# An attention and feed-forward kernel on one Trainium2 core: the second projection of five of six token blocks with w_out as the stationary operand

## The chip, the cores and the metric

The kernel runs on one core of one Trainium2 chip. The metric is the device time of the whole program in microseconds (us); lower is better. TensorE (PE) multiplies matrices: each matmul holds one operand, the stationary one, which a weight load (PEld) brings in, and lets the columns of the other, the moving one, stream past; the sums go to PSUM, which has eight banks of 512 fp32 columns. VectorE (DVE), ScalarE (ACT) and GpSimd (POOL) work on tiles, SyncE (SP) issues most DMA transfers. Each engine runs its own queue in order and waits on semaphores of the others.

## The reference

```python
def _attn_ref(r, k, v, w, u):            # B, H, S, D = 4, 8, 768, 48
    for t in range(S):
        cur = np.einsum('bhd,bhe->bhde', u[None] * kt, vt)
        y[:, :, t] = np.einsum('bhd,bhde->bhe', rt, state + cur)
        state = w[None, :, :, None] * state + np.einsum('bhd,bhe->bhde', kt, vt)

def _moe_ref(x, w_in, w_out):            # x 3072 x 384, w_in 384 x 2048, w_out 2048 x 384
    h = x @ w_in
    g = np.where(h > 0.0, h, np.exp(np.minimum(h, 0.0)) - 1.0)
    return g @ w_out
```

x is y with the heads joined: 3072 tokens (4 sequences of 768) of 384 columns. The output is 3072 x 384, fp32.

## The kernel before

The tokens are cut into six blocks n = 0 to 5 (NCH): 128 tokens of each of the four sequences b, so T = 512 columns a block. The hidden columns are cut into 16 chunks f (NF) of 128. `start` (L303) does the attention of block 0 by an order written out by hand (START, L39); then `run` (L294) makes 96 steps (n, f), each by `step` (L384) in the hand-written order FIRST (block 0, L51) or LATER (the rest, L55). Within an engine the instructions stand in the order in which these lists call them.

A step (n, f) holds:
- `hidden` (L933, "hid"): nine matmuls into one of two PSUM banks `ps_h`: three parts c of the 384 input columns, and for each the products (wh, xh), (wh, xl), (wl, xh), since every fp32 operand is held as two fp32r parts, a rounded one and the rest. The stationary operand is w_in, the moving one has 512 columns.
- `negative` and `elu` (L946, L954; "neg" on ScalarE, "elu" on VectorE), then `split_g` ("gh" on ScalarE, "gl" on VectorE), which give the two parts of g.
- `project` (L967, "proj") of an earlier step: one step back in block 0 and in the first steps of block 1, two later. It makes twelve matmuls, three products for each of the four sequences b: the stationary operand is a 128-token part of g, the moving one has the 384 columns of w_out, and each sequence adds up in a PSUM bank of its own, `acc0` to `acc3`.
- a piece of the attention of block n+1 or n+2: a unit (one sequence of one block) is spread over four steps and more by stages. "A" (`scores`, L686) and "Y" (`outputs`, L792) are its matmuls; "Dp" and "Dq" (`diag_scores`, L702) are products on GpSimd, "pa" and "pb" (`take_scores`, L720) take the scores on VectorE, "dk" and "dr" (L636 to L651) turn PSUM into rk on VectorE, "t" (`turn_blocks`, L581) is a transposition in 32 x 32 blocks on VectorE, "kr" (L668) and "ru" (L653) are products.
- in block 0 also the preparation of weight chunk k = f + 2: "ma" and "mb" (`merge`, `sign`, L535 and L544, VectorE) join the words of two stages into `wide`; "sp" (`split_w`, L555) is one ScalarE copy of 768 columns, w_out (i = 0) and w_in (i = 1) together, into the rounded part `wh`; "r3" (`rest_w`, L559) takes the rest of w_out on GpSimd, "r4d" that of w_in on VectorE. In START, sp:1, rs:0 and rsd:1 are the same operations for chunk 1, chunk 0 and chunk 1's w_out, in that order in the list.

At the end of the step after a block's last projection `store` (L983) empties the four accumulators, two copies on VectorE and two on ScalarE, into `o`, and SyncE issues four transfers of 128 rows of 1,536 bytes each. The last block's four transfers are issued by ScalarE.

PSUM holds `acc0` to `acc3`, two `ps_h` banks and two banks `rw` for the attention (`bank`, L238); in `start` the six banks outside `ps_h` take turns.

## Time and profile before

| | us |
|---|---|
| median of 3 runs (516.57 to 517.32) | 517.2 |
| the profiled execution, device time | 517.24 |
| its span, first to last instruction | 515.4 |

| engine | busy us | share of the span |
|---|---|---|
| PE (matmuls) | 501.9 | 97% |
| DVE | 302.3 | 59% |
| ACT | 257.8 | 50% |
| POOL | 118.8 | 23% |

The granted clock of TensorE was 0.998 of full speed in this execution, so 2.4 GHz nearly throughout. Matmuls overlap, and their ends are modelled; so the time that a matmul takes in a stream is read from the distance of starts in the timeline, not from its listed length. DMA packets filled 45% of the 16 DMA engines' span.

### The profile page before, as it was taken

The page shows a single profiled execution, that of the slowest core. Times are in us where ns is not written, and L with a number is a line of the kernel's source. Part 1 is how long each engine was busy: PE and PEld are TensorE (multiplying, and loading weights), DVE is VectorE, ACT ScalarE, POOL GpSimd, SP SyncE. Part 2 cuts the span into 40 slices and gives each one's busy share as a digit, 9 for nine tenths or more (in the row PEclk, how much of TensorE's full clock was granted, in tenths as well). Part 3 has the DMA queues.
Part 4 walks back from the last instruction along what each step waited for, and adds up shares of the span by engine and source line. Part 5 has one row for each costly group of instructions (what it writes and reads, how often), then busy time and mean ns, then how long its engine had stood idle before and what let it go on. Part 6 is the DMA issues. An engine that isn't in the chain of part 4 may idle for free.

```text
span 515.4 us, 9327 instructions
## 1 busy us (share of the span) xinstructions
PE 501.9 (97%) x3568; PEld 442.1 (86%) x3568; DVE 302.3 (59%) x523; ACT 257.8 (50%) x486; POOL 118.8 (23%) x135
## 2 busy tenths in 40 slices
PE   8989999999999999999999999999999999999995
PEld 6888888978888888888888888888888888999995
DVE  6799999995475465564454654654654542433331
ACT  2279888773553543635535435435445354444442
POOL 7732222243322321303303303122022020000000
PEclk9999999999999999999999999999999999999999
DMA  9996779745643551724614634345266200100001
GB/s 134 209 179 157 168 152 228 152 109 148 123 111 66 96 117 29 185 52 88 135 48 92 132 105 96 80 67 126 51 149 135 62 31 8 50 14 1 0 1 66
DMA packets 105562, 50.92 MB, mean 99 GB/s; under 512 B 80162, under 2 KB 101412, under 8 KB 105508
## 3 DMA queue, kind: packets, MB, share of 16 engines
q1 hardware_dynamic: 104932, 49.44, 44.7%
q10 hardware_dynamic: 576, 0.79, 0.4%
q8 instruction: 30, 0.49, 0.4%
q14 instruction: 24, 0.20, 0.1%
HBM read 35.13 MB, written 13.11 MB: 94 GB/s over the span
## 4 chain that ended last, share of the span: by engine, by line
PE 80%; DVE 6%; DMA 5%; ACT 4%; SPq 3%; issue 1%; POOL 0%; DVEq 0%; ACTq 0%
PE ps_acc L978 35%; PE ps_h L941 33%; PE ps_a L696 4%; PE ps_y L811 4%; DMA stage<-in_moe_w_in_dram 3%; PE ps_y L805 2%; SPq L860 1%; DVE wide L539 1%; DMA raw<-in_k_dram 1%; PE ps_y L825 1%; ACT stage L531 1%; DVE wide L547 1%; PE ps_y L751 1%; DVE ps_h L956 1%; DMA stage<-in_moe_w_out_dram 1%
## 5 line engine op out<-in xcount | busy, mean ns | idle before, releaser
L978 PE MATMUL ps_acc<-wh,g 128*128 128x384 f32 x768 | 215.9, 342 | 0.1
L941 PE MATMUL ps_h<-x,wh 128*128 128x512 f32 (+1 forms) x588 | 180.0, 388 | 0.1
L978 PEld LDWEIGHTS ps_acc<-wh,g 128*128 128x128 f32 x768 | 140.8, 188 | 6.9 <-DVE stage L992 0.8
L978 PE MATMUL ps_acc<-wl,g 128*128 128x384 f32 x384 | 129.8, 338 | 0.0
L956 DVE SCALAR_TENSOR_TENSOR ps_h<-g,ps_h 128x512 f32<-128x512 f32 x96 | 66.7, 695 | 104.9 <-ACT g L951 104.5
L941 PEld LDWEIGHTS ps_h<-x,wh 128*128 128x128 f32 x588 | 107.9, 188 | 16.7 <-DVE ps_h L956 0.4
L941 PE MATMUL ps_h<-x,wl 128*128 128x512 f32 (+1 forms) x294 | 114.2, 389 | 0.0
L950 ACT ACTIVATE g<-ps_h 128x512 f32<-128x512 f32 x96 | 57.6, 600 | 92.4 <-PE ps_h L941 92.4
L964 DVE TENSOR_TENSOR g<-ps_h,g 128x512 fp32r<-128x512 f32 x96 | 66.2, 689 | 39.1 <-ACT g L962 38.5
L962 ACT CAST g<-ps_h 128x512 fp32r<-128x512 f32 x96 | 56.1, 584 | 58.3 <-DVE ps_h L956 58.2
L978 PEld LDWEIGHTS ps_acc<-wl,g 128*128 128x128 f32 x384 | 72.2, 188 | 2.1
L941 PEld LDWEIGHTS ps_h<-x,wl 128*128 128x128 f32 x294 | 55.2, 188 | 11.9
L951 ACT ACTIVATE g<-g 128x512 f32<-128x512 f32 x96 | 60.8, 634 | 3.1
L715 POOL TENSOR_TENSOR a<-ident,diag 128x512 f32<-128x512 f32 x21 | 24.3, 1159 | 125.1 <-DVE diag L666 75.6
L722 DVE COPY_PREDICATED a<-mask,ps_a 128x512 f32<-128x512 int32 x40 | 29.0, 735 | 31.9 <-PE ps_a L696 31.9
L850 ACT CAST x<-ps_y 128x256 fp32r<-128x256 f32 x40 | 13.0, 376 | 66.9 <-PE ps_y L825 51.6
L673 POOL TENSOR_TENSOR k_t<-k_t,rev 128x384 f32<-128x384 f32 x12 | 12.2, 1017 | 109.2 <-PE ps_y L805 80.8
L564 POOL TENSOR_TENSOR wl<-wide,wh 128x384 fp32r<-128x384 f32 x16 | 16.8, 1051 | 46.6 <-ACT wh L557 46.4
L711 ACT ACTIVATE a<-ident,diag 128x128 f32<-128x128 f32 x76 | 24.2, 394 | 0.0
L840 DVE TENSOR_TENSOR state<-sw,ps_y 48x192 f32<-48x192 f32 x32 | 11.2, 351 | 20.1 <-ACT x L850 19.7
L811 PE MATMUL ps_y<-a,v_t 128*64 128x128 f32 x320 | 21.9, 279 | 0.0
L615 POOL TENSOR_TENSOR rk<-rk,pw 128x512 f32<-128x512 f32 x16 | 19.1, 1192 | 8.1 <-DMA rk<-blocks 8.1
(107 smaller groups left out, 420.2 us busy)
## 6 DMA issues: line engine op xcount, KB each, us to landing
blocks<-tb SPq DMA_DIRECT2D x64, 128.0 KB, 2.3
rk<-blocks SPq DMA_DIRECT2D x16, 512.0 KB, 3.5
stage<-in_moe_w_out_dram SPq DMA_DIRECT2D x16, 384.0 KB, 5.0
stage<-in_moe_w_in_dram SPq DMA_DIRECT2D x32, 144.0 KB, 4.5
r_t<-in_r_dram SPq DMA_DIRECT2D x22, 192.0 KB, 4.3
k_t<-in_k_dram SPq DMA_DIRECT2D x22, 192.0 KB, 5.0
v_t<-in_v_dram SPq DMA_DIRECT2D x22, 192.0 KB, 5.3
out_dram<-stage SPq DMA_DIRECT2D x20, 192.0 KB, 2.1
```

The lines of the kernel that those rows point to most:

```text
L696: self.nc.tensor.matmul(pa[i][:, a * P : (a + 1) * P], lhsT=kw[rows, a, :], rhs=rw[rows, a, :], start=True, stop=True,)
L711: self.nc.scalar.activation(un["a"][i][:, a, :], self.ident, AF.Copy, scale=diag[:, a : a + 1])
L715: self.nc.gpsimd.tensor_mul(un["a"][i], self.ident.unsqueeze(1).to_broadcast([P, HP, P]), diag.unsqueeze(2).to_broadcast([P, HP, P]),)
L722: self.nc.vector.copy_predicated(un["a"][i], self.mask.bitcast(I32).unsqueeze(1).to_broadcast([P, HP, P]), un["pa"][i].rearrange("p (a t) ...
L811: nc.tensor.matmul(y, lhsT=v[:, h * D : h * D + DP], rhs=un["a"][h % 2][:, h // 2, :], start=(n == 0 and s == 0), stop=(s == 1), skip_grou ...
L941: self.nc.tensor.matmul(ph[:, part], lhsT=a[:, c * P : (c + 1) * P], rhs=x[:, c, part], start=(c == 0 and i == 0), stop=(c == NC - 1 and i ...
L950: nc.scalar.activation(g, ph, AF.Relu, scale=-1.0)
L951: nc.scalar.activation(g, g, AF.Exp, scale=-1.0)
L956: self.nc.vector.scalar_tensor_tensor(ph, g, -1.0, ph, op0=ALU.add, op1=ALU.max)
L962: nc.scalar.copy(part, g)
L964: nc.vector.tensor_sub(part, g, self.g[n, f][2].bitcast(F32))
L978: self.nc.tensor.matmul(self.acc[n][b][:, 0:DM], lhsT=a[:, at], rhs=w, start=(f == 0 and i == 0), stop=(f == NF - 1 and i == 2),)
```

## The change

The projection of blocks 0 to 4 swaps its operands: a 128-column part of w_out is stationary, g moves with 512 columns. There are three accumulators (one for each 128 output columns) instead of four, nine matmuls a step instead of twelve, and the sums come out with output columns on the partitions. Block 5 (`by_tokens`) keeps the old form, with its fourth accumulator in an `rw` bank. Three `rw` banks take the place of two.

So that a transposition in 32 x 32 blocks on VectorE puts whole runs of 96 output columns together, the columns of w_out are regrouped when it is split: `split_w` becomes a GpSimd copy of w_out (384 columns, runs of 32) and a ScalarE copy of w_in (384 columns). GpSimd's copy stands in its queue where "sp" is called, ahead of Dp, "r3" and, in START, of rs:0. Block 5 reads w_out as the moving operand with the regrouping undone, in runs of 32 columns.

`store` of blocks 0 to 4 is one ScalarE copy of `acc1` (512 columns) to `o_raw`, and three VectorE transpositions of 512 columns: of `acc0`, of `acc2`, and of `o_raw`. The stores go out as sixteen transfers of 48 KB with runs of 384 bytes, four at the end of each of the next four steps (`store_next`).

```diff
     def bank(self, kind):
-        tag, bufs = "rw", 2
+        tag, bufs = "rw", 3
         if self.all_banks:
-            tag = ("rw", "rw", "acc0", "acc1", "acc2", "acc3")[self.bank_n % 6]
-            bufs = 1 if tag.startswith("acc") else 2
+            tag = ("rw", "rw", "rw", "acc0", "acc1", "acc2")[self.bank_n % 6]
+            bufs = 1 if tag.startswith("acc") else 3
...
+        self.store_next()
         if last[1] == NF - 1 and last[0] in self.acc:
             self.store(last[0])
...
     def split_w(self, k):
-        if k <= NF:
-            self.nc.scalar.copy(self.pairs[k][0], self.place(self.wide, k, WIDE).bitcast(F32))
+        if k > NF:
+            return
+        for i, copy in enumerate((self.nc.gpsimd.tensor_copy, self.nc.scalar.copy)):
+            if self.has(k, i):
+                copy(*(self.grouped(t, i) for t in (self.weight(k, i)[0], self.joined(k, i))))
...
+    def grouped(self, t, i):
+
+        if i == 1:
+            return t
+        if t.dtype == F32R:
+            return t.rearrange("p (c i d) -> p c i d", c=NC, i=4)
+        return t.rearrange("p (i c d) -> p c i d", c=NC, i=4)
...
     def project(self, n, f):
...
-        for b in range(B):
-            at = slice(b * P, (b + 1) * P)
+        for j, acc in enumerate(self.acc[n]):
             for i, (a, w) in enumerate(((gh, wh), (gh, wl), (gl, wh))):
+                if by_tokens:
+                    at, lhs = acc[:, 0:DM], a[:, j * P : (j + 1) * P]
+                    rhs = w.rearrange("p (c i d) -> p i c d", c=NC, i=4)
+                else:
+                    at, lhs, rhs = acc, w[:, j * P : (j + 1) * P], a
                 self.nc.tensor.matmul(
-                    self.acc[n][b][:, 0:DM], lhsT=a[:, at], rhs=w,
+                    at, lhsT=lhs, rhs=rhs,
                     start=(f == 0 and i == 0), stop=(f == NF - 1 and i == 2),
                 )
...
+        o = self.o.rearrange("p (j c d) -> p c j d", j=T // 32, c=NC)
+        nc.scalar.copy(self.o_raw, acc[1])
+        for c, src in ((0, acc[0]), (2, acc[2]), (1, self.o_raw)):
+            nc.vector.transpose(o[:, c], src.rearrange("p (j t) -> p j t", t=32))
+        self.to_store = [(n, b) for b in range(B)]
...
+    def store_next(self):
+        if not self.to_store:
+            return
+        n, b = self.to_store.pop(0)
+        o = self.o.rearrange("p (b j d) -> p b j d", b=B, j=4)[:, b]
+        out = self.out.rearrange("(b n j t) (i d) -> n b i t j d", b=B, n=NCH, j=4, i=4)[n, b]
+        for i in range(4):
+            self.nc.sync.dma_start(out[i], o[i * 32 : (i + 1) * 32])
```

## Rows read from the trace of the kernel before

**Rows 1.** The page's first part: busy us, share of the span, instructions of an engine.

```profile
PE 501.9 (97%) x3568; PEld 442.1 (86%) x3568; DVE 302.3 (59%) x523; ACT 257.8 (50%) x486; POOL 118.8 (23%) x135
```

**Rows 2.** Busy time in stretches of 20 us: a stretch of block 0, one of block 2, one of block 5. Columns: length, then busy us (and instructions) of PE, PEld, DVE, ACT, POOL, the granted clock, the DMA share, GB/s.

```profile
80.00:100.00 20.00, 19.62 (x149) 17.11 (x149) 18.83 (x32) 17.77 (x30) 5.62 (x5) 1.00 0.90 180
...
220.00:240.00 20.00, 20.00 (x149) 17.71 (x148) 10.86 (x19) 8.89 (x18) 4.97 (x5) 1.00 0.43 88
...
460.00:480.00 20.00, 20.00 (x103) 18.23 (x102) 6.58 (x10) 8.72 (x15) 0.00 (x0) 1.00 0.00 1
```

**Rows 3.** Timeline of PE in block 5: the first row is the first of a step's twelve projection matmuls, the second the first of the next nine hidden ones, the third the fourth of these, the last the first matmul of the next projection. Columns: start, length, engine, line, operation, count; a row may join several matmuls.

```profile
469.86 0.33 PE L978 MATMUL ps_acc<-wh,g 128*128 128x384 f32 x1
...
471.95 0.62 PE L941 MATMUL ps_h<-x,wh 128*128 128x512 f32 x2
...
472.65 0.62 PE L941 MATMUL ps_h<-x,wh 128*128 128x512 f32 x2
...
474.01 0.33 PE L978 MATMUL ps_acc<-wh,g 128*128 128x384 f32 x1
```

**Rows 4.** Timeline of PE in block 1, a projection that follows attention matmuls (first and second matmul), the hidden matmuls after it, and the next projection.

```profile
128.58 0.44 PE L978 MATMUL ps_acc<-wh,g 128*128 128x384 f32 x1
128.87 0.34 PE L978 MATMUL ps_acc<-wl,g 128*128 128x384 f32 x1
...
130.79 0.63 PE L941 MATMUL ps_h<-x,wh 128*128 128x512 f32 x2
...
132.88 0.33 PE L978 MATMUL ps_acc<-wh,g 128*128 128x384 f32 x1
```

**Rows 5.** Groups of instructions by line and shape, whole span: count, busy us and mean ns of one, idle us of the engine before it and what ended that.

```profile
L564 POOL TENSOR_TENSOR wl<-wide,wh 128x384 fp32r<-128x384 f32 x16 | 16.8, 1051 | 46.6 <-ACT wh L557 46.4
...
L585 DVE STREAM_TRANSPOSE tb<-r_t 128x512 f32<-128x512 f32 x16 | 11.2, 702 | 0.0
...
L134 POOL MEMSET state<- 128x256 f32 x3 | 0.8, 312 | 0.0
...
L504 ACT COPY pwt<-ps_pt 128x512 f32<-128x512 f32 x1 | 0.6, 587 | 0.5 <-PE ps_pt L502 0.5
```

**Rows 6.** Timelines at the ends of blocks 1, 3 and 4: the two VectorE copies of the store, and the PE rows of the first projection of the next block (for block 1's end also the third row, which holds the wait, and the start of what follows).

```profile
211.46 1.01 DVE L992 COPY stage<-ps_acc 128x384 f32<-128x384 f32 x2
...
211.33 0.33 PE L978 MATMUL ps_acc<-wh,g 128*128 128x384 f32 x1
...
211.68 0.83 PE L978 MATMUL ps_acc<-wh,g 128*128 128x384 f32 x2
...
213.75 0.62 PE L941 MATMUL ps_h<-x,wh 128*128 128x512 f32 x2
...
373.01 1.01 DVE L992 COPY stage<-ps_acc 128x384 f32<-128x384 f32 x2
...
373.11 0.33 PE L978 MATMUL ps_acc<-wh,g 128*128 128x384 f32 x1
...
448.39 1.01 DVE L992 COPY stage<-ps_acc 128x384 f32<-128x384 f32 x2
...
449.09 0.33 PE L978 MATMUL ps_acc<-wh,g 128*128 128x384 f32 x1
```

**Rows 7.** Timelines at the end of `start`: "mb" of chunk 1 on VectorE, rs:0 on GpSimd, and the third matmul of the first hidden half on PE, the first one that reads rs:0's result.

```profile
29.74 0.94 DVE L547 SCALAR_TENSOR_TENSOR wide<-stage,wide 128x768 int32<-128x768 int32 x1
...
30.05 1.50 POOL L564 TENSOR_TENSOR wl<-wide,wh 128x384 fp32r<-128x384 f32 x1 [1.51 <-ACT wh L557]
...
32.23 0.29 PE L941 MATMUL ps_h<-x,wl 128*128 128x256 f32 x1
```

**Rows 8.** Timelines of `start` (first three rows: GpSimd, then the same VectorE form twice, first beside that GpSimd product and later without one) and of block 0 around steps (0, 12) and (0, 13): VectorE, GpSimd and PE.

```profile
24.64 1.27 POOL L625 TENSOR_TENSOR a<-a,mask 128x512 f32<-128x512 f32 x1 [1.22 <-ACT a L624]
...
24.71 1.61 DVE L539 SCALAR_TENSOR_TENSOR wide<-stage 128x384 int32<-128x384 int32 x1
...
112.39 0.55 DVE L539 SCALAR_TENSOR_TENSOR wide<-stage 128x384 int32<-128x384 int32 x1
...
101.15 0.94 DVE L547 SCALAR_TENSOR_TENSOR wide<-stage,wide 128x768 int32<-128x768 int32 x1
...
104.41 0.55 DVE L673 TENSOR_TENSOR k_t<-k_t,rev 128x384 f32<-128x384 f32 x1
...
107.44 0.70 DVE L956 SCALAR_TENSOR_TENSOR ps_h<-g,ps_h 128x512 f32<-128x512 f32 x1
...
101.38 1.62 POOL L715 TENSOR_TENSOR a<-ident,diag 128x512 f32<-128x512 f32 x1 [3.11 <-DVE diag L666]
103.05 1.02 POOL L564 TENSOR_TENSOR wl<-wide,wh 128x384 fp32r<-128x384 f32 x1
...
104.04 1.16 PE L696 MATMUL ps_a<-rk 48*128 48x128 f32 x16 [0.38 <-DVE rk L627]
```

**Rows 9.** Timelines near the end of block 0: "pb" on VectorE, and the "Y" matmuls that wait for it.

```profile
109.88 0.69 DVE L722 COPY_PREDICATED a<-mask,ps_a 128x512 f32<-128x512 int32 x1
...
110.63 0.65 PE L805 MATMUL ps_y<-rk,state 48*64 48x128 f32 x12 [0.68 <-DVE a L722]
```

**Rows 10.** Timeline of SyncE's queue after the end of block 1, and its next work.

```profile
216.00 1.99 SPq L997 DMA_DIRECT2D out_dram<-stage  x4
...
225.23 1.77 SPq L594 DMA_DIRECT2D blocks<-tb  x4
```

More of the change, by code (lines that the diff above doesn't have):

```diff
@@ L227, in arm @@
             self.bank_n = 0
+            self.to_store = []
             self.all_banks = True
@@ L231, in arm @@
             self.wide = self.wk.tile([P, 2 * WIDE, DM], I32, tag="wide", name="wide")
+            o = self.late.bitcast(F32).rearrange("p s d w -> p (s d w)")
+            self.o, self.o_raw = o[:, 0 : B * DM], o[:, B * DM : B * DM + T]
             if general:
@@ L453, in step @@
                     todo[name](m, b)
+        self.store_next()
         if last[1] == NF - 1 and last[0] in self.acc:
             self.store(last[0])
-        if (n, f) == (0, NF - 1):
-            o = self.late.bitcast(F32).rearrange("p s d w -> p (s d w)")[:, 0 : B * DM]
-            self.o = o.rearrange("p (b d) -> p b d", b=B)
     def warm(self, times):
@@ L555, in split_w, with has, joined @@
     def split_w(self, k):
-        if k <= NF:
-            self.nc.scalar.copy(self.pairs[k][0], self.place(self.wide, k, WIDE).bitcast(F32))
+        if k > NF:
[3 more added lines that the diff above has]
+                copy(*(self.grouped(t, i) for t in (self.weight(k, i)[0], self.joined(k, i))))
+    def has(self, k, i):
+        return k <= NF and not (k == 0 and i == 0) and not (k == NF and i == 1)
+    def joined(self, k, i):
+        return self.wide[:, 2 * (k % WIDE) + i].bitcast(F32)
+    def grouped(self, t, i):
[4 more added lines that the diff above has]
+        return t.rearrange("p (i c d) -> p c i d", c=NC, i=4)
     def rest_w(self, k, i, eng=None):
-        if k > NF or (k == 0 and i == 0) or (k == NF and i == 1):
+        if not self.has(k, i):
             return
-        hi, lo = self.weight(k, i)
-        a = self.wide[:, 2 * (k % WIDE) + i].bitcast(F32)
+        hi, lo = (self.grouped(t, i) for t in self.weight(k, i))
+        a = self.grouped(self.joined(k, i), i)
         (eng or self.nc.gpsimd).tensor_sub(lo, a, hi.bitcast(F32))
@@ L969, in project @@
         wh, wl = self.weight(f + 1, 0)
+        by_tokens = n + 1 == NCH
         if f == 0:
+            tags = [(f"acc{c}", 1) for c in range(NC)] + [("rw", 3)] * by_tokens
             self.acc[n] = [
-                self.ps.tile([P, 512], F32, tag=f"acc{b}", name=f"ps_acc{b}", bufs=1)
-                for b in range(B)
-            ]
-        for b in range(B):
-            at = slice(b * P, (b + 1) * P)
+                self.ps.tile([P, 512], F32, tag=tag, name=f"ps_acc{i}", bufs=bufs)
+                for i, (tag, bufs) in enumerate(tags)
+            ]
+        for j, acc in enumerate(self.acc[n]):
             for i, (a, w) in enumerate(((gh, wh), (gh, wl), (gl, wh))):
+                if by_tokens:
[3 more added lines that the diff above has]
+                    at, lhs, rhs = acc, w[:, j * P : (j + 1) * P], a
                 self.nc.tensor.matmul(
-                    self.acc[n][b][:, 0:DM], lhsT=a[:, at], rhs=w,
+                    at, lhsT=lhs, rhs=rhs,
                     start=(f == 0 and i == 0), stop=(f == NF - 1 and i == 2),
@@ L984, in store @@
         nc = self.nc
-        moves = []
-        for b, po in enumerate(self.acc.pop(n)):
-            if self.general:
-                o = self.wk.tile([P, DM], F32, tag="o", name="o", bufs=2)
-            else:
-                o = self.o[:, b, :]
-            if b % 2:
-                nc.vector.tensor_copy(o, po[:, 0:DM])
-            else:
-                nc.scalar.copy(o, po[:, 0:DM])
-            row = b * S + n * P
-            if self.general or n + 1 < NCH:
-                nc.sync.dma_start(self.out[row : row + P, :], o)
-                continue
-            moves.append((self.out[row : row + P, :], o))
-            if b != 1:
-                for dst, src in moves:
-                    nc.scalar.dma_start(dst, src)
-                moves = []
+        acc = self.acc.pop(n)
+        if n + 1 == NCH:
+            moves = []
+            for b, po in enumerate(acc):
+                o = self.o.rearrange("p (b d) -> p b d", b=B)[:, b]
+                if b % 2:
+                    nc.vector.tensor_copy(o, po[:, 0:DM])
+                else:
+                    nc.scalar.copy(o, po[:, 0:DM])
+                row = b * S + n * P
+                moves.append((self.out[row : row + P, :], o))
+                if b != 1:
+                    for dst, src in moves:
+                        nc.scalar.dma_start(dst, src)
+                    moves = []
+            return
[4 more added lines that the diff above has]
+        self.to_store = [(n, b) for b in range(B)]
+        while self.general and self.to_store:
+            self.store_next()
+    def store_next(self):
+        if not self.to_store:
+            return
+        n, b = self.to_store.pop(0)
[3 more added lines that the diff above has]
+            self.nc.sync.dma_start(out[i], o[i * 32 : (i + 1) * 32])
 @with_exitstack
```

## The prediction

> **What bounds the kernel now.** I read the page's busy shares first: PE is busy 97% of the span, the next engine 59% [rows 1]. The table of stretches then shows that this is no average of unlike stages on PE's side: from block 1 on PE is busy for all 20.00 us of a stretch, while VectorE has half its time free (10.86 us in block 2, 6.58 in block 5) [rows 2]. In block 0 two engines are close together: PE 19.62, VectorE 18.83 us of 20 [rows 2]. There the timeline shows who waits: the scores "A" of step (0, 13) begin at 104.04, 0.38 us after PE ran dry, and what released them was VectorE [rows 8]. So block 0 goes at VectorE's pace up to "Y" of its last unit, which again waits for VectorE, 0.68 us [rows 9]. After that every matmul that gets shorter shortens the kernel, and every wait put in front of one lengthens it. The granted clock is 1.00 in all these stretches (2.4 GHz) [rows 2], and PE's idle time stays far too small for me to expect a change of level.
>
> **The sum is made against the profiled execution:** 517.24 us, of which 515.4 are span; it lies 0.04 above the median of the runs, so I make no correction.
>
> **Projection, on the path.** The columns do not change: 12 x 384 = 9 x 512 = 4608. What changes is the fixed part of each matmul. In block 5 twelve matmuls take 469.86 to 471.95, 2.09 us, 0.174 each; nine hidden ones take 471.95 to 474.01, 2.06 us. Of these the first three need 0.70 (0.233 each), the last six 1.36 (0.227 each) [rows 3]. Against 0.160 and 0.213 us for the bare columns at 2.4 GHz that is 0.014 us a matmul once the stream has settled, and a little more in the first few after a change of form. After attention matmuls the same projection takes 128.58 to 130.79, 2.21 us, of which 0.12 are in its first interval (0.29 instead of 0.17), and the hidden group after it 2.09 [rows 4].
> Lower bound of the gain: the new projection is as long as a hidden group, 2.06, and 2.18 after a switch: 0.03 us in either kind of step. Upper bound: with one form of matmul throughout nothing has to settle, and all run at 0.227: projection and hidden 2.04 each, so 4.15 becomes 4.08 in a plain step, and 4.30 becomes 4.20 after a switch; the mean is 0.085. I take 0.06, between the ends, since the hidden rows settle after a few matmuls of their own. It counts in the 64 steps of blocks 1 to 4 and in the last three of block 0: 67 x 0.06 = **-4.0 us** (-2.0 to -5.7). In the other 13 steps of block 0 VectorE sets the pace, and I count nothing.
> The Trainium skill (TensorE: Matmul & The Clock Gate, Back-to-back issue gap) gives columns / 2.4 + 2.5 ns. By it three matmuls fewer would be worth 0.0075 us a step and the whole term 0.5 us. The rows speak against it: 0.174 and 0.227 us are 11 ns and more above it, and the distance is the same for both widths.
>
> **The store at the ends of blocks 1 to 4, on the path.** At the end of block 1 the two VectorE copies start at 211.46 and take 1.01; PE starts the next block's projection at 211.33, runs into the second bank, which the first copy holds until about 212.0, and ends at 213.75: 2.42 instead of 2.09, so 0.33 of wait and restart [rows 6]. From 212.0 its nine remaining matmuls take 1.75 where 9 x 0.174 = 1.57 would do, so 0.18 is the restart. After the change the first bank, which the first matmul wants, is freed by a transposition that VectorE can begin no earlier than 211.46, because its queue up to there hangs on "Y" two steps back and not on the projection. One of 512 columns takes 0.70 from SBUF [rows 5]; from PSUM no row shows one; I take 0.70, with 0.5 (half of the two copies) and 1.0 as ends. The bank is free at 212.16, and the projection ends at 212.16 + 0.18 + 2.06 = 214.40: +0.65. The end of block 2 has the same work in the same order: +0.65. At block 3 the copies start at 373.01 and PE comes at 373.11 [rows 6]: free at 373.71, end at 375.95 instead of 373.11 + 2.09 = 375.20: +0.75. At block 4 they start at 448.39 and PE comes at 449.09 [rows 6]; there the transposition ends just as PE arrives: +0.2. Block 0's end costs nothing: a "Y" stands between, and the projection comes at 128.58 only [rows 4]. The gain of the two steps ahead of each wait, counted above, is lost in it: 4 x 0.1. Together **+2.65 us** (+1.8 to +3.6). Behind the transpositions stands the next "elu": three take 2.1 us where the copies took 1.01, so it comes up to 1.1 us later. Its g is wanted two steps on, some 8 us, which covers that; without this cover it would cost up to 1.1 at each end.
>
> **The split on GpSimd, at the end of `start`.** rs:0 on GpSimd began at 30.05 and took 1.50 [rows 7]; now the copy of chunk 1's w_out stands ahead of it, and that waits for "mb", which ends at 29.74 + 0.94 = 30.68 [rows 7]. The trace has no GpSimd copy. The nearest rows are a memset (312 ns for 256 columns, so 0.47 us for 384) and a subtraction of 384 columns (1.05 us) [rows 5]; I take 0.65, nearer the memset, since a copy reads one operand and not two. rs:0 would end at 30.68 + 0.65 + 1.05 = 32.38; the third matmul, at 32.23 until now [rows 7], needs it and a weight load first: **+0.4 us** (+0.15 to +0.8). PE's delay goes on to "elu" and from there to VectorE, which is not ahead at this point.
> The Trainium skill (GPSIMD Engine Reference, Engine selection) calls one-input operations on GpSimd roughly line-rate; an estimate by that page would be 0.5 us a copy, the lower end, and the sum would be 0.6 us less. No run here shows it yet.
>
> **The split on GpSimd, in block 0.** VectorE and GpSimd stand in each other's way: the same form took 1.61 us beside a GpSimd product that ran from 24.64 to 25.91, and 0.55 alone [rows 8]. Both of its operands lie in SBUF; forms with one operand in PSUM I take as free. In step (0, 12) "mb" ends at 101.15 + 0.94 = 102.09. GpSimd would then do the copy (to 102.74), the product Dp (1.62 beside "mb" in these rows; some 1.1 now that it runs beside forms with PSUM operands; to 103.85) and "r3" (1.02; to 104.87). Until now "r3" ended at 104.07, and "kr" (two SBUF operands) began on VectorE at 104.41 [rows 8]; now it would wait until 104.87. The next "elu" at 107.44 comes 0.15 us after VectorE was last free, so about 0.35 of the 0.46 arrive there, and at the next "A". Three units pay that in full, the first, which `start` delays anyway, 0.1: **+1.15 us** (+0.5 with a copy of 0.47, +2.6 with one of 1.05).
>
> **A third `rw` bank, at "Y" of block 0's last unit.** PE waited there for the second bank of the scores, which "pb" frees; the rest of the "Y" matmuls on the state took 0.65 after it [rows 9]. With three banks they can go before "pb" is done: **-0.5 us** (0 to -0.6).
>
> **Counted at nothing.** ScalarE loses half of "sp" in block 0 and has 2.2 of 20 us free there [rows 2]; VectorE, which sets the pace, does not get shorter by it. SyncE issues sixteen transfers for four: four took 1.99 us, and its queue was then idle from 217.99 to 225.23 [rows 10]; twelve of the sixteen fit before the next `blocks`, the last four go behind that step's work, and nothing waits for them until the next block's end. If a store held up `blocks`, it would be by less than 2 us of a chain that has steps to spare. Block 5's moving w_out in runs of 32 columns: 0, with a rival below.
>
> **The sum:** 517.24 - 4.0 + 2.65 + 0.4 + 1.15 - 0.5 = 516.9 us.
>
> **Rivals.** (1) Forecast: what TensorE gains is about what the store and the split cost. 516.9, within 0.2% either way (a bit over 1 us, which is about what a measurement of this kernel can tell from no change). Chance 0.37. (2) The stream does settle: 0.085 a step, 5.7 us in all. For it: the last six hidden intervals [rows 3]; against it: the group after a switch keeps a mean of 0.232 to its end [rows 4]. 516.9 - 1.7 = 515.2. Chance 0.33. (3) GpSimd's copy is as slow as its subtraction, 1.05 us, and VectorE's two-operand work in block 0 waits for GpSimd in every unit: 0.8 + 2.6 in place of 0.4 + 1.15, so 518.8. It ends slower by over 0.2% from a copy of about 1.0 us on, since each 0.1 us more costs 0.1 in `start` and 0.3 in block 0. For it: the 1.61 us row [rows 8]; against it: memset's rate [rows 5]. Chance 0.22. (4) The regrouped moving operand streams worse, so that the change does to block 5 what it says it does not: 10% on 192 matmuls of 0.174 is 3.3 us, 520.2. No row shows a 384-column operand in runs. Chance 0.05. (5) The fixed part is not paid per matmul, so that nine take what twelve took and the change does not do what it says: gain 0, 520.9. That 0.014 us stands on top of both widths [rows 3] speaks against it. Chance 0.03. The Trainium skill's page on TensorE comes close to this case (above).
>
> **Range and chances.** 514.6 to 519.2 us takes in (1) to (3) with their bounds and leaves out (4), (5) and the case in which all ends fall on the good side. Faster by over 0.2%: 0.33 (2). Within 0.2%: 0.37 (1). Slower by over 0.2%: 0.30 (3 to 5).
>
> **What the profile would show.** Projection: nine matmuls of 512 columns, starts 0.227 to 0.233 us apart; a plain step of blocks 1 to 4 takes 4.08 to 4.12 instead of 4.15. Store: the first projection of blocks 2, 3 and 4 preceded by a wait of 0.6 to 1 us on a VectorE transposition, that of block 5 by some 0.1. Split: GpSimd's copy at 0.5 to 0.8 us; the first hidden half held at its third matmul; "kr" in block 0 at about 1 us instead of 0.55. Block 5: twelve matmuls in 2.09 us as before. The prediction is wrong if the copy takes over 1 us, if plain steps keep 4.15, or if the banks are freed before PE asks for them.

## The result and the profile after

The changed kernel takes 520.79 us (median of six runs, 520.45 to 522.32) where the kernel before took 517.12 beside it: ratio 1.0076, 95% interval 1.0060 to 1.0093, slower by 3.7 us. The forecast was 516.9. The profiled execution took 520.45 us, of which 518.7 are span. Its first hidden half starts 0.8 us later than before's (32.71 against 31.91). Executions scatter there, so it is not counted below: in another execution of the changed kernel (run `changed` below) the same half starts at 31.69, in an execution of the kernel before without stores at 32.24.

I laid PE's matmuls of both traces side by side, line by line, and noted where the distance between them changes. The stretches in which it does, in order:

| where | forecast, us | trace, us |
|---|---|---|
| end of `start` (split on GpSimd) | +0.4 | +0.13 |
| block 0, waits for the scores | +1.15 | +0.80 |
| projection and hidden, block 0 up to there | 0 | -0.33 |
| block 0, "Y" of the last unit (third bank) | -0.5 | -0.71 |
| hidden (1, 0), waits for the fills of x | 0 | +0.92 |
| block 1, scores behind the stores in SyncE's queue | 0 | +0.55 |
| ends of blocks 1 to 4 | +2.65 | +2.51 |
| projection and hidden, blocks 1 to 4 | -4.0 | -0.85 |
| block 5 | 0 | +0.35 |

These add up to 3.4 us. (With the 0.8 of the start, less a wait of 0.39 at 357 us that only before's execution had, and less a tail behind the last matmul that is 0.56 shorter, that is the 3.2 by which the two spans differ.) The ends of the blocks came as forecast; the gain that was to pay for them did not come. First the plain step. These are PE's rows in block 2, one projection and the hidden group behind it; start and length in us:

```profile
234.38 0.39 PE L1001 MATMUL ps_acc<-g,wh 128*128 128x512 f32 x1
234.61 0.39 PE L1001 MATMUL ps_acc<-g,wl 128*128 128x512 f32 x1
234.83 0.64 PE L1001 MATMUL ps_acc<-g,wh 128*128 128x512 f32 x2
235.31 0.39 PE L1001 MATMUL ps_acc<-g,wl 128*128 128x512 f32 x1
...
236.46 0.63 PE L958 MATMUL ps_h<-x,wh 128*128 128x512 f32 x2
...
238.52 0.39 PE L1001 MATMUL ps_acc<-g,wh 128*128 128x512 f32 x1
```

From 234.38 to 236.46 the nine projections take 2.075 us, the nine hidden ones to 238.52 take 2.065. [rows 3] had 2.092 and 2.061. The starts in the first three rows lie 0.23 and 0.22 apart, but the pair that starts at 234.83 takes 0.48 until 235.31. So the stream is even up to the third matmul, and then it isn't. Four steps (one unit) of blocks 2 and 3 take 17.02 us of hidden and projected groups, before 17.07: 0.05 x 16 units, with the last steps of block 0, is the -0.85 of the table.

The end of block 1, first PE, then VectorE (to be compared with [rows 6]):

```profile
212.98 0.40 PE L958 MATMUL ps_h<-x,wl 128*128 128x512 f32 x1
214.20 0.47 PE L1001 MATMUL ps_acc<-g,wh 128*128 128x512 f32 x1 [0.83 <-DVE stage L1028]
...
216.35 0.63 PE L958 MATMUL ps_h<-x,wh 128*128 128x512 f32 x2
...
213.35 1.30 DVE L1028 STREAM_TRANSPOSE stage<-ps_acc 128x512 f32<-128x512 f32 x2
214.57 0.67 DVE L1028 STREAM_TRANSPOSE stage<-stage 128x512 f32<-128x512 f32 x1
```

PE is ready at 213.21 (212.98 and a matmul of 0.23) and waits for the first of the two transpositions that begin at 213.35. The next hidden begins at 216.35, 3.14 us after PE was ready, where before's projection took 2.42: 0.72 us for this end, forecast 0.65. The two from PSUM take 1.30, so the price of 0.70 was right as well.

SyncE's queue in block 1, and the wait that comes of it:

```profile
129.69 3.34 SPq L611 DMA_DIRECT2D blocks<-tb  x4
...
138.49 3.94 SPq L877 DMA_DIRECT2D x<-x  x6
142.48 8.76 SPq L1040 DMA_DIRECT2D out_dram<-stage  x16
151.34 1.82 SPq L611 DMA_DIRECT2D blocks<-tb  x4
...
161.14 1.05 PE L713 MATMUL ps_a<-rk,tb 48*128 48x128 f32 x14 [0.33 <-POOL tb L632]
```

All sixteen stores stand behind the six fills and go out together, 8.76 us of issuing; `blocks` of the next unit waits behind them until 151.34. Before, it went out at 146.44, and no store stood ahead of it. GpSimd turns it into the scores' operands, and PE waits. How long is up to the execution. In the eight traces of programs with all sixteen stores in this place the hidden group ahead of these scores takes 0.13 to 1.81 us longer than before's 2.15 (0.40 here, 1.81 in `changed`); in the four with the stores spread out (below) and in the one without stores it is at most 0.005. First SyncE in the kernel before, then PE in `changed`:

```profile
146.44 1.78 SPq L594 DMA_DIRECT2D blocks<-tb  x4
...
162.18 1.16 PE L713 MATMUL ps_a<-rk,tb 48*128 48x128 f32 x16 [1.73 <-POOL tb L632]
```

GpSimd's copy and the subtraction behind it (columns as in [rows 5]):

```profile
L581 POOL TENSOR_TENSOR wl<-wide,wh 128x384 fp32r<-128x384 f32 x16 | 16.3, 1018 | 0.9
...
L560 POOL CAST wh<-wide 128x384 fp32r<-128x384 f32 x16 | 8.1, 505 | 56.0 <-DVE wide L547 56.0
```

The copy takes 0.505 us, below the 0.65 that the sum used.

And what became of the third bank in block 0, SyncE and PE:

```profile
111.25 1.95 SPq L611 DMA_DIRECT2D blocks<-tb  x4
116.18 0.34 SPq L616 DMA_DIRECT2D rk<-blocks  x1
116.61 3.80 SPq L877 DMA_DIRECT2D x<-x  x6
...
120.45 0.73 PE L958 MATMUL ps_h<-x,wh 128*128 128x512 f32 x2 [0.65 <-DMA x<-x]
```

"Y" no longer waits 0.68 us for "pb" [rows 9], but ten microseconds later hidden (1, 0) waits for the fills. These stand in SyncE's queue behind `rk<-blocks`, which hangs on VectorE's transpositions; with VectorE 1.3 us later than before, PE had nothing to gain by coming earlier.

### The profile page after: what moved, and what is told of

Its sections match the earlier page's. It is cut to its first block, busy times and chain, and to the rows that moved or that the text cites. A ratio compares the mean times of both kernels' runs of the same rounds, so it can differ in the third digit from the quotient of the medians.

```text
span 518.7 us, 8918 instructions
## 1 busy us (share of the span) xinstructions
PE 503.3 (97%) x3328; PEld 411.0 (79%) x3328; DVE 306.4 (59%) x528; ACT 252.1 (49%) x480; POOL 123.5 (24%) x151
## 4 chain that ended last, share of the span: by engine, by line
PE 71%; DVE 9%; DMA 7%; SPq 4%; ACT 3%; issue 3%; POOL 1%; DVEq 0%; ACTq 0%; POOLq 0%
PE ps_acc L1001 31%; PE ps_h L958 30%; DMA stage<-in_moe_w_in_dram 4%; PE ps_a L713 3%; PE ps_y L828 3%; SPq L877 2%; PE ps_y L822 2%; DVE wide L539 1%; DVE ps_h L973 1%; DVE wide L547 1%; PE ps_y L768 1%; DMA stage<-in_moe_w_out_dram 1%; DVE x L869 1%; ACT stage L531 1%; DMA blocks<-tb 1%
## 5 line engine op out<-in xcount | busy, mean ns | idle before, releaser
L1001 PE MATMUL ps_acc<-g,wh 128*128 128x512 f32 x480 | 167.8, 404 | 2.3 <-DVE stage L1028 2.3
L958 PEld LDWEIGHTS ps_h<-x,wh 128*128 128x128 f32 x588 | 109.2, 188 | 24.9 <-DMA x<-x 1.1
L1001 PEld LDWEIGHTS ps_acc<-g,wh 128*128 128x128 f32 x480 | 90.0, 188 | 26.1 <-ACT g L967 2.5
L1001 PE MATMUL ps_acc<-g,wl 128*128 128x512 f32 x240 | 94.2, 392 | 0.0
L1001 PEld LDWEIGHTS ps_acc<-g,wl 128*128 128x128 f32 x240 | 45.2, 188 | 8.4
L732 POOL TENSOR_TENSOR a<-ident,diag 128x512 f32<-128x512 f32 x21 | 21.9, 1045 | 114.6 <-PE ps_h L958 49.3
L1001 PE MATMUL ps_acc<-wh,g 128*128 128x384 f32 x128 | 35.2, 339 | 0.0
L1001 PEld LDWEIGHTS ps_acc<-wh,g 128*128 128x128 f32 x128 | 23.4, 188 | 1.0 <-issue 0.4
```

The lines of the kernel that those rows point to most:

```text
L732: self.nc.gpsimd.tensor_mul(un["a"][i], self.ident.unsqueeze(1).to_broadcast([P, HP, P]), diag.unsqueeze(2).to_broadcast([P, HP, P]),)
L958: self.nc.tensor.matmul(ph[:, part], lhsT=a[:, c * P : (c + 1) * P], rhs=x[:, c, part], start=(c == 0 and i == 0), stop=(c == NC - 1 and i ...
L1001: self.nc.tensor.matmul(at, lhsT=lhs, rhs=rhs, start=(f == 0 and i == 0), stop=(f == NF - 1 and i == 2),)
```

## The experiments

Theory A, drawn from these rows: the stream of matmuls gained next to nothing; the ends of the blocks, SyncE's queue and block 0 are the loss. Rivals: GpSimd's part of the split is the main loss (B), or block 5's regrouped operand is (C). Every ratio below is to the kernel before, run on the same chip (its medians there 518.2 to 518.4).

**Store order.** ScalarE copies the bank that PE wants first; VectorE transposes the others.

```diff
-        nc.scalar.copy(self.o_raw, acc[1])
-        for c, src in ((0, acc[0]), (2, acc[2]), (1, self.o_raw)):
+        nc.scalar.copy(self.o_raw, acc[0])
+        for c, src in ((1, acc[1]), (2, acc[2]), (0, self.o_raw)):
```

> Edit: at the ends of blocks 1 to 4 ScalarE copies the first bank (which the next block's projection wants first) and VectorE transposes the second and third at once and the first from the copy; in the changed kernel it is the second bank that is copied. Theory A (the trace of the changed kernel: the matmul stream gained only about 0.75 us in all, and the waits for the first bank at four block ends cost 0.72 + 0.77 + 0.76 + 0.26 = 2.5 us): the copy ends at 212.69 in block 1, before PE asks at 213.44, so the waits go and the time falls by 2 to 2.5 us, to 518.3 to 518.8. Rival B (GpSimd's part of the split is what costs): 520.8 less under 0.5. Rival C (the regrouped moving operand of block 5 is what costs): 520.8, too.

Measured: 0.9998 (0.9981 to 1.0016), so nearly all of the loss is gone. (From 1.0076 that is some 4 us, more than the 2 to 2.5 expected; the trace below accounts for 2.5, and the intervals just leave room for that. The wait behind SyncE's stores, 1.10 here and 1.81 in `changed`, differs between the executions as well.) The end of block 1 in its trace, ScalarE, PE, VectorE:

```profile
213.25 0.59 ACT L1026 COPY stage<-ps_acc 128x512 f32<-128x512 f32 x1
...
214.31 0.39 PE L1001 MATMUL ps_acc<-g,wh 128*128 128x512 f32 x1
214.49 1.30 DVE L1028 STREAM_TRANSPOSE stage<-ps_acc 128x512 f32<-128x512 f32 x2
...
214.76 0.99 PE L1001 MATMUL ps_acc<-g,wh 128*128 128x512 f32 x2
...
216.74 0.63 PE L958 MATMUL ps_h<-x,wh 128*128 128x512 f32 x2
```

The copy is done at 213.84, before PE comes at 214.31. What is left is a short wait for the second bank (0.99 for two matmuls instead of 0.62), as in the kernel before. From 214.31 to the next hidden it takes 2.43 us, 0.71 less than the changed kernel; over the four ends the hidden and projected groups take 2.5 less.

**Stores in two of four steps.**

```diff
-        self.store_next()
+        if f % 4 in (1, 2):
+            self.store_next()
```

> Edit: the four stores of one row block (4 transfers each) go out in two of every four steps, behind the six fills, so that 8 transfers and not 16 stand ahead of the next `blocks`. Theory A: in block 1 `blocks` then goes out about 4 us earlier, the wait of 0.40 us for the scores at 161.1 and the two small ones behind it (0.07 + 0.08) vanish; 520.3. Rival (the lateness comes from VectorE's transposes of t5, 129.69 instead of 127.23, and the stores only lie in a gap): the wait stays, 520.8. B and C: 520.8.

Measured: 1.0050 (1.0033 to 1.0067), 1.3 us under the result's ratio, where 0.5 was expected. Its trace, SyncE and PE:

```profile
142.96 4.08 SPq L1041 DMA_DIRECT2D out_dram<-stage  x8
148.57 2.56 SPq L612 DMA_DIRECT2D blocks<-tb  x4
...
161.39 0.83 PE L714 MATMUL ps_a<-rk,tb 48*128 48x128 f32 x10
```

Eight stores go out, `blocks` follows 2.8 us earlier, and the scores wait for nobody. That the lateness came from VectorE alone (the rival) is refuted: the unit's first `blocks` went out at 130.27 here, no earlier than 129.69 above.

**The split on ScalarE again.** `(nc.scalar.copy, nc.scalar.copy)` in `split_w`.

> Edit: ScalarE makes the grouped copy of w_out in the split, GpSimd none. Theory A: GpSimd's copy takes 0.505 us and costs 0.13 us at the end of start and at most 0.8 in block 0 (the two larger waits for the scores, 0.20 + 0.60): 519.9 to 520.7, or above if ScalarE's own two copies come later. Rival B (VectorE and GpSimd in each other's way is the main loss, as in the prediction's third rival): 1.5 us or more come back, 519.3 or less, and the wait for `x<-x` at 120.45 goes with it.

Measured: 1.0083 (1.0062 to 1.0103), no better than the changed kernel, so as a cure it fails. Its trace does not price GpSimd's copy cleanly, though. "kr" is back at 0.55 us, but block 0's waits for the scores stay (1.9 us in all, 1.7 in the changed kernel, 1.0 before), and now VectorE waits longer for ScalarE, which makes both copies (0.22 and 0.75 us ahead of "gl", 0.13 and 0.66 before). B falls by the table and by `swap`, which took back most of the loss and left the split as it was.

**Block 5's operand in stored order.** The last four copies put the columns in order instead.

```diff
-                    rhs = w.rearrange("p (c i d) -> p i c d", c=NC, i=4)
+                    rhs = w
```

> Edit: in block 5 the moving w_out is read in its stored order (384 columns in a row), and the four last copies put the columns in order. Theory A: hidden and projected groups of block 5 take 2.061 and 2.092 us again instead of 2.082 and 2.098, 13 steps and more: -0.35 us, and the last copies may give some of it back; 520.4 to 520.8. Rival C (the operand in runs costs more than the trace shows, as in the prediction's fourth rival): 517.5 to 519.5.

Measured: 1.0067 (1.0038 to 1.0095). In its trace hidden and projected groups of block 5 take 2.060 and 2.093 us again, 0.027 less a step. C is true at the size of the trace, 0.35 us, and no more.

**The stream by itself.**

> A kernel that leaves out all of the computation and runs only fp32r matmuls in sections of 90: 512 columns, 384, 256, 384 in runs of 32, 5 groups of nine of 512 and twelve of 384 in turn, and then 512 and 384 beside VectorE and ScalarE, and 512 again; the stationary matrix changes with each matmul as in the kernel. As predicted (0.014 us for each matmul whatever its width, settling in a uniform stream): 0.227, 0.174 and 0.121 us apart for 512, 384 and 256 columns, the mixed groups longer at each change. Theory P (what stands on top grows with the columns): 0.231, 0.174 and 0.117; then twelve of 384 and nine of 512 take the same, and the projection could gain nothing. Theory N (other engines' work stretches the intervals): 512 columns at 0.216 to 0.227 in the quiet sections and at 0.231 beside VectorE and ScalarE. The Trainium skill's rule (TensorE: Matmul & The Clock Gate, Back-to-back issue gap: columns / 2.4 + 2.5 ns) gives 0.216, 0.163 and 0.109. 384 in runs of 32: as 384 in a row, or up to 1% longer.

PE in its trace; from one start to the next, divided by 90:

```profile
52.37 20.56 PE L51 MATMUL k<-mv,st 128*128 128x512 f32 x90
72.77 15.79 PE L56 MATMUL k<-mv,st 128*128 128x384 f32 x90
88.39 10.95 PE L61 MATMUL k<-mv,st 128*128 128x256 f32 x90
99.18 15.77 PE L67 MATMUL k<-mv,st 128*128 128x384 f32 x90
114.78 2.23 PE L73 MATMUL k<-mv,st 128*128 128x512 f32 x9
```

0.2267, 0.1736 and 0.1199 us for 512, 384 and 256 columns: 0.0132 to 0.0136 on top of the bare columns at every width. So the forecast's fixed part is real, and an even stream does run at 0.227; P (it grows with the columns) falls. Beside VectorE and ScalarE it was 0.2271, so N (their work stretches it) falls. Nine of 512 and twelve of 384 in turn took 2.08 and 2.11. The Trainium skill's rule (TensorE: Matmul & The Clock Gate, Back-to-back issue gap), which the page gives for a matmul by itself, would give 0.216, 0.163 and 0.109; this trace is 11 ns above it at each width.

**Without stores,** before and changed: what the rest of the change is worth.

> The kernel before without the copies and stores of blocks 0 to 4 (those rows of the output are not written). In its trace the first projections of blocks 2, 3, 4 and 5 wait 0.33, 0.33, 0.3 and 0 us for a copy: 1.0 us less than the kernel before, ratio 0.998.

> The changed kernel without the copies, transpositions and stores of blocks 0 to 4 (those rows of the output are not written). What is left of the change is the projection, the split and block 5. As predicted (-4.0 - 0.4 of projection, +0.4 + 1.15 of split, -0.5 of the third bank): 3.3 us less than the kernel before without stores, ratio to the kernel before 0.992. Theory A (projection -0.75, block 5 +0.35, start +0.13, block 0 +0.1 to +0.9): 0.2 us less to 0.6 more than the kernel before without stores, ratio to the kernel before 0.9975 to 0.999.

Measured: 0.9992 (0.9981 to 1.0004; 0.4 us gained, 1.0 expected) and 0.9990 (0.9973 to 1.0008). Without stores the change is worth nothing, as theory A has it; the 3.3 us of the forecast are outside.

**The banks of before.**

> The changed kernel with the banks of before: two of `rw`, and acc3 beside acc0 to acc2. As predicted (the third bank is worth 0.5 us at "Y" of block 0's last unit): 0.5 us more than the changed kernel. Theory A (the 0.71 us that it saved there are given back at 117.6, where hidden (1, 0) waits for the fills of x, which hang on VectorE and SyncE and not on PE): as the changed kernel, within 0.3 us; in the trace "Y" waits 0.7 us longer and the fills 0.7 us less.

Measured: 1.0070 (1.0046 to 1.0094), as the changed kernel. In its trace "Y" takes 1.39 us longer, while block 0's three waits for the scores before it are 0.76 shorter and the fills' wait 0.08. What the banks and what the execution does to block 0 can't be told apart by that; in the time the third bank is worth nothing.

**What unsettles the stream.** The question was now why the changed kernel's groups don't take 2.04.

> A kernel that leaves out all of the computation: groups of nine matmuls of 512 columns into one bank and nine into three banks, in turn, as hidden and project of the changed kernel, with 36 even ones between the sections. In the changed kernel the stream is even (226, 227) at the start of project, then 237, 241, 224, 226, 229, 232, 233 ns, and settles only in the next hidden: 0.06 us lost per step, and the gain of the uniform stream with it. Section 1: nothing else. Section 2: moving and stationary tiles in the order of the kernel. Section 3: ScalarE reads the bank of each group of nine when it is full, so that the ninth matmul signals. Section 4: the same over two banks only, so that the first matmul also waits on ScalarE. Section 5: beside a GpSimd product from SBUF. Theory S (the signal, or the wait, unsettles the stream): sections 1, 2 and 5 at 2.04 us for nine, sections 3 and 4 (or 4 alone) at 2.06 to 2.08. Theory O (the order of operands, or the change of bank within project): section 2 (or 1 and 2) at 2.06 to 2.08. Theory G (GpSimd's reads): section 5 alone.

All sections: 2.040 for nine. S (signals and waits), O (order and banks) and G (GpSimd's reads) fall.

> A kernel that leaves out attention, weights and stores: six sections of steps of nine matmuls of 512 columns into the bank h and nine into three banks, with 36 even ones between the sections. Section 1: ScalarE's Relu and Exp behind each hidden group; 2: and VectorE's elu in place in the bank; 3: and ScalarE's gh; 4: and VectorE's gl; 5: and project moves gh and gl of two steps before, so that it waits for them; 6: and the three banks are added to through the whole section. None of the things tried in the run before moved the nine matmuls from 2.04 us, while the changed kernel's project takes 2.075 and its hidden 2.065. Theory V (VectorE's work in PSUM beside the stream): 2.04 in section 1, 2.06 or more from section 2 or 4 on. Theory W (operands that other engines have just written, or the wait for them): 2.04 up to section 4, 2.06 or more in 5 and 6. Theory C (what is left: adding to banks over steps, or something outside these steps): 2.04 up to section 5, or in all six.

2.040 in all six sections but for one restart behind a wait. V (VectorE's work in PSUM) and W (operands just written) fall too; something of the kernel's own had to be left.

> The changed kernel, with other arithmetic in some half blocks, so that its output is not the reference's: block 2, first half: the three gl products behind the six others; second half: gl first in each bank; block 3, first half: project moves x instead of g; second half: project always has the w_out of chunk 0 stationary; block 4, first half: hidden always has the w_in of chunk 1 stationary; second half: hidden's nine in another order (three wh and xh, three wh and xl, three wl and xh); block 5: projection by columns too, its store by transpositions. Theory L (the first use of gl unsettles the stream): the long pair (237, 241) moves to the seventh matmul in block 2's first half and to the first in its second half, and is gone in block 3's first half. Theory M (the stationary matrices): it is gone or elsewhere in block 3's second half or block 4. Theory E (other engines' attention work): it is gone in the last steps of block 5, where none is left, and these take 2.04 and 2.04. Theory D (something of the chip outside all that): the same pair at the same place in all of them.

With the three gl products last (block 2, first half), the six others were even and the long intervals began with the seventh; with gl first they began with the first. Where project moved x instead of g (block 3, first half) plain steps were even:

```profile
316.67 0.39 PE L1012 MATMUL ps_acc<-x,wh 128*128 128x512 f32 x1
...
318.71 0.61 PE L966 MATMUL ps_h<-x,wh 128*128 128x512 f32 x2
...
320.75 0.39 PE L1012 MATMUL ps_acc<-x,wh 128*128 128x512 f32 x1
```

2.04 and 2.04. Other stationary matrices, another order of hidden's nine and a block 5 without attention work left the pattern where it was. Theory L holds: it is gl. What of it? No profile shows addresses; in the memory map of the compiled program the three gl tiles start 64 bytes past a multiple of 128 (192 past one of 256), behind two `diag` tiles of 32 bytes, and gh, x and the weights at a multiple (128 past one of 256).

> A kernel that leaves out all of the computation: nine matmuls of 512 columns into one bank and nine into three in turn, five times a section, with 36 even ones between the sections; every third matmul of the second nine moves another slice, which starts 0, 32, 64, 128 and 256 bytes past a multiple of 128 in sections 1 to 5. Section 6: all operands of the eighteen moved from 64 bytes past. Section 7: the stationary matrix of the second nine 64 bytes past. Theory T (the start address modulo 128 of the moving operand): sections 1, 4 and 5 even at 2.04 for nine; 2 and 3 with a long pair behind each change, 2.06 to 2.09; 6 even but for its ends, or all slower; 7 even. Rivals (values, writer or change of tile): all even.

PE in its trace; project-like and hidden-like groups in turn, a third of the first moved from 32 (84.88), 64 (113.91), 128 (142.77) and 256 bytes off (171.43):

```profile
84.88 2.25 PE L37 MATMUL acc<-mv,st 128*128 128x512 f32 x9
86.96 2.25 PE L37 MATMUL h<-mv,st 128*128 128x512 f32 x9
89.05 2.25 PE L37 MATMUL acc<-mv,st 128*128 128x512 f32 x9
...
113.91 2.24 PE L37 MATMUL acc<-mv,st 128*128 128x512 f32 x9
115.98 2.23 PE L37 MATMUL h<-mv,st 128*128 128x512 f32 x9
118.05 2.24 PE L37 MATMUL acc<-mv,st 128*128 128x512 f32 x9
...
142.77 2.22 PE L37 MATMUL acc<-mv,st 128*128 128x512 f32 x9
144.83 2.20 PE L37 MATMUL h<-mv,st 128*128 128x512 f32 x9
146.87 2.22 PE L37 MATMUL acc<-mv,st 128*128 128x512 f32 x9
...
171.43 2.20 PE L37 MATMUL acc<-mv,st 128*128 128x512 f32 x9
173.47 2.20 PE L37 MATMUL h<-mv,st 128*128 128x512 f32 x9
175.51 2.20 PE L37 MATMUL acc<-mv,st 128*128 128x512 f32 x9
```

Worked out from the start times of both traces, ns between one start and the next:

```
changed kernel, project  227 226 237 241 224 226 229 232 233   2075
changed kernel, hidden   231 236 228 232 231 227 227 226 227   2065
64 bytes off, project    227 227 236 241 224 226 229 233 232   2075
64 bytes off, hidden     231 236 228 233 231 226 227 227 226   2065
128 bytes off            227 227 234 226 226 234 226 227 234   2061, then 2039
0 or 256 bytes off       227 227 226 227 227 226 227 227 226   2040, then 2040
```

The kernel's pattern comes back at 64 bytes, each interval to a nanosecond. But theory T had the modulus wrong: 128 bytes off costs 8 ns at each such matmul, 256 nothing. A stationary matrix 64 bytes off costs as well, where T had it even (2.102 for the nine, 2.051 for the next). And with all moving operands 64 bytes off, the stationary ones in place, every group takes 2.060 and is uneven throughout, though no moving operand differs from the next; so it is not only a change between moving operands that counts. (The operands called in place start 128 bytes past a multiple of 256 in all these programs; whether another common place does as well is not shown.) The run `aligned` moved gl to a multiple of 128:

```diff
-        un["diag"] = self.wk.tile([P, H], F32, tag="diag", name="diag", bufs=2)
+        un["diag"] = self.wk.tile([P, 2 * H], F32, tag="diag", name="diag", bufs=2)[:, 0:H]
```

> Edit: `diag` of 16 columns instead of 8 (8 used), so that gl starts at a multiple of 128 bytes in SBUF. Theory T: project and hidden of blocks 1 to 4 take 2.04 each in plain steps instead of 2.075 and 2.065, and 0.25 us less in each four steps (the sum over block 3's first half of the run before): 4.0 us less than the changed kernel in all, ratio to the kernel before 1.000 (0.998 to 1.002). Rivals: 1.008 as the changed kernel.

> The same edit to the kernel before, where gl is stationary in the projection and w_out moves. Theory T: no change (ratio 0.999 to 1.001), since every moving operand started at a multiple of 128 already. Rival (the stationary operand's address counts, too): its 384-column groups get shorter, ratio 0.995 or less.

Measured: `aligned` 1.0036 (1.0019 to 1.0053), half of what T expected: gl was now 128 bytes off, and project and hidden took 2.061 and 2.039. `before_aligned` 1.0026 (1.0016 to 1.0036), slower instead of unchanged: its steps take 2.106 + 2.081 instead of 2.092 + 2.061. The stationary gl's place counts, and 64 bytes off was better there than 128.

**The changed kernel mended.** First the edits of `swap`, `spread` and `block5` together, with the changed kernel itself on the same chip, then the same with gl at a multiple of 128, and last with `4 * H` in place of `2 * H`, which puts gl at the same place modulo 256 as gh, x and the weights.

> The edits of the runs swap, spread and block5 together. Theory A: 2.5 of the block ends, 0.57 of block 1 (and the 0.70 that swap's trace shows at 158.6) and 0.37 of block 5 come off the changed kernel: 3.4 to 4.1 us less, ratio to the kernel before 0.996 to 1.000. Rival (the waits only move on, since block 1's chain over SyncE and VectorE is the bound behind them): not better than swap alone, ratio 1.000.

> The changed kernel once more, on the same chip as the experiments: ratio to the kernel before 1.006 to 1.009 if chips agree.

> The edits of swap, spread, block5 and aligned together: theory T adds 4.0 us to what the run best gave (ratio 0.9987): 512.5 to 514 us on this scale, ratio 0.990 to 0.993. Rival (block 1's and block 0's waits take up what the stream gives): ratio 0.995 or more.

> The edits of swap, spread and block5, and `diag` of 32 columns (8 used), so that gl starts 128 bytes past a multiple of 256 as gh, x and the weights do. Theory T256: project and hidden of blocks 1 to 4 take 2.040 each in plain steps; four steps take 0.25 us less than in the run best, 4.0 us in all, and block 5, where gl is stationary, is no longer than in best: ratio to the kernel before 0.989 to 0.992 (513 us). Rivals: the waits of blocks 0 and 1 take it up, as in aligned_best (0.9965); or the pattern stays (0.9987 as best).

Measured: `best` 0.9987 (0.9971 to 1.0002); `changed` 1.0084 (1.0065 to 1.0104); `aligned_best` 0.9965 (0.9946 to 0.9984), short of the 0.990 to 0.993 expected, with gl still 128 bytes off (2.060 and 2.040); `even_best` 0.9912 (0.9885 to 0.9939), 513.88 us (513.26 to 514.66) where the kernel before had 518.35. It beats both kernels. PE in block 2 of its trace:

```profile
232.56 0.39 PE L1002 MATMUL ps_acc<-g,wh 128*128 128x512 f32 x1
...
234.60 0.62 PE L959 MATMUL ps_h<-x,wh 128*128 128x512 f32 x2
...
236.64 0.39 PE L1002 MATMUL ps_acc<-g,wh 128*128 128x512 f32 x1
```

2.04 and 2.04. Four steps take 16.78 us against 17.02 in the changed kernel and 17.07 before.

## Why the prediction was wrong

**The step that failed is the size of the projection's term, -4.0 us, measured -0.85.** Its reasoning was sound up to "with one form of matmul throughout nothing has to settle": the fixed part is paid per matmul (0.0132 to 0.0136 us at three widths), and an even stream runs at 0.227. Its own sign of being wrong came true: a plain step took 4.14 us, hardly less than the 4.15 before, where it had 4.08 to 4.12. What it did not ask is whether the stream would be of one form. The change makes gl a moving operand, and gl's tile lay 64 bytes off the others, so each step has a new disturbance in place of the two changes of width that it lost. With gl in its place the gain is there: 17.07 to 16.78 in four steps, 0.073 us a step, between the 0.06 taken and the upper bound of 0.085. No row of the trace of before could have shown it, since gl did not move in that kernel; but the bound from below (0.03 a step) was taken from a row, and the true value (0.013) lay under it. That bound assumed that the new projection would be as long as a hidden group; the range was too narrow there.

**The fifth rival** (gain 0, 520.9, chance 0.03) came nearest to the time, for a wrong reason: it had the fixed part not paid per matmul, which `stream` refutes.

**The ends of the blocks** (+2.65, trace +2.51) were right in place, order and size; `swap` shows it, since freeing the first bank by a copy takes back that much and perhaps more. The 0.4 us of gain lost in the waits was no loss, because there was no gain.

**The split** (+0.4 and +1.15) was too dear. The copy took 0.505 us, where the Trainium skill's sentence (GPSIMD Engine Reference, Engine selection) had led to 0.5; the trace agrees with it. At the end of `start` it cost 0.13: the first hidden half takes 1.38 us instead of 1.25, and 1.24 in `split`. In block 0 "kr" took 0.65 us instead of 0.55 beside "r3" and the elu behind it came 0.15 later, some 0.25 in each of two units. A third delay has another source: at 88.86 ScalarE waits 0.37 us for a weight transfer, and "ma" at 90.70 on VectorE comes 0.35 later by it; whether the change delays that transfer stays open. And 0.33 of the 0.80 only took back what block 0's own matmul groups had gained.

**The third bank** (-0.5, trace -0.71) was right at its place, and given back 10 us later. The prediction looked at the wait that goes and not at what is late next: the fills, which hang on VectorE.

**Counted at nothing** failed for SyncE. "Twelve of the sixteen fit before the next `blocks`" held at the end of block 1 (twelve went out in one go behind the fills, then idle time), but not in block 1 for block 0's stores, where fills and stores came four microseconds later and all sixteen stood ahead of `blocks`. It cost 0.55 us in this execution and up to 1.8 in others; the forecast had "less than 2 us of a chain that has steps to spare", while `blocks` went out 4.9 us later than before, and PE itself was only 1.4 late there. Block 5's operand, also counted at nothing, cost 0.35; the fourth rival had the mechanism at ten times the size. Why runs of 32 columns lengthen the hidden group behind them is open; in `stream` such a section by itself ran at 0.1733.

## What to carry to other kernels

A change of operands moves tiles into roles that the trace of before has not tried: before counting on an even stream of matmuls, ask where each moving and stationary tile starts in SBUF (the on-chip memory that holds them), try the same place modulo 256 bytes, and measure it; here a padding of 192 bytes in all took the ratio from 0.9987 to 0.9912, some 3.9 us. When an accumulator has to be emptied before the next block, give the first copy to the engine that reaches it first and let the slow operation work from the copy. And when a wait disappears, follow the next thing in that chain to its own queue before booking the gain.

## What the runs showed of the hardware

- Matmuls of this stream (fp32r, a weight load before each) start 0.0132 to 0.0136 us later than their bare columns at 256, 384 and 512 columns alike, and at 512 neither semaphores, changes of bank, readers of the banks nor other engines' work moved that by more than 0.0005.
- After a change of width, and behind a moving operand that starts 32 or 64 bytes off the others modulo 256, the starts are uneven (224 to 241 ns around 227); at 64 bytes they are even again from the sixth matmul of the next group. At 128 bytes only the matmul itself takes 8 ns longer; 256 bytes change nothing.
- A stationary matrix 64 bytes off, with the moving operands in place, cost more than a moving one (2.102 against 2.075 for nine of 512). In the kernel before, where twelve of 384 and nine of 512 take turns, the same offset of the stationary gl was better (2.092 + 2.061) than 128 bytes or none (2.106 + 2.081, in `before_aligned` and in block 5 of `even_best`). So an offset can also help, and has to be measured.
- Transpositions of 512 columns take VectorE the same time from PSUM (1.30 us for two) as from SBUF (0.67 for one).
